# An mLSTM cell with a GELU feed-forward block: a later place for the second chunk's gates, a finer order on ScalarE, and one mask on GpSimd

## The chip, the cores and the metric

The kernel runs on one core of a Trainium2 chip. The core has five engines that run side by side, each through its own list of instructions in order: TensorE (PE in the profile; PEld is its loading of weights), VectorE (DVE), ScalarE (ACT), GpSimd (POOL), and SyncE (SP), which here issues nearly all DMAs. [...] The metric is the device time of one execution in microseconds (us); lower is better.

## The reference

The input is q, k, v and an output gate of shape (4 batches, 8 heads, 768 steps, 40), and two scalar gates per head and step. The reference walks over the steps:

```
m_new  = max(f + m, i)
f_stab = exp(f + m - m_new);  i_stab = exp(i - m_new)
C = f_stab * C + i_stab * outer(v, k);   n = f_stab * n + i_stab * k
y = sigmoid(o) * (C q) / max(|n.q|, 1)
```

Then y is put into rows of 320 (8 heads of 40) for 3072 tokens, and a feed-forward block follows: h = x @ w_in (320 x 2048), g = h * sigmoid(1.702 h), out = g @ w_out (2048 x 320). All is fp32.

## The kernel before

The 768 steps are cut into 6 chunks (w = 0 to 5) of L = 128 steps. Within a chunk the recurrence is turned into attention. From the gates come running sums and running maxima; from these an L x L matrix of weights per head, exp(...) below a causal mask; the scores k.q are multiplied by it (L352), and the product with v gives the values (L362). A state per head carries what came before the chunk. `seam` transposes a batch's rows to x (L404, L405); then come `up` (x @ w_in, GELU) and `down` (@ w_out). The loop over w at L761 does chunk w's feed-forward block and puts the attention of chunk w+1 between its matmuls.

The order is written by hand (`manual_schedule`): each engine gets its instructions in the order of the Python calls. PSUM tiles of the attention come from a pool of four (`ps_a`), so an instruction of TensorE can also wait until an older tile has been read.

Chunk 0 is special, since nothing runs beside it:

- `gates(w)` (L249) does the scan, the running maximum `m_run` and the columns derived from it on VectorE, on [32, 128] tiles. For w > 0 it also issues the DMA that writes `m_row` to DRAM (L269). For chunk 1 it is called at L686, after the transposes of batch 1. Its inputs are loaded by `load_gates(1)`, third in the list of first loads (L170).
- `weights(0, b)` (L319) builds the exponents in PSUM for four heads at a time: a matmul of the identity with `not_yet` puts a large negative number above the diagonal (L324), two small bf16 matmuls per head add the terms (L328, L329), and ScalarE takes the exponential (L330).
- `convert(n)` (L223) turns piece n of the weights, loaded as 64-bit words, into fp32: two ScalarE operations of 128 x 512 (L228 on the high words, L229 on the low ones) and four of VectorE (L232 to L237), the last of which needs L229. Pieces 0 to 9 are w_in, 10 to 19 w_out. The pieces pass through the rooms of `big`; `fetch(n)` issues their DMAs, and piece 16 takes the room of piece 10.

Chunk 1 and later take their weights by another way: `spread(w)` (L312) reads `m_row` back with four broadcasting DMAs of 512 KB into the `wt` tiles, ScalarE takes the exponentials (L334), and GpSimd masks them with `affine_select` (L336). `load_blocks(w, 0)` and `(w, 1)` load k and q in 16 small DMAs each, for VectorE's 32 x 32 transposes (L301).

`beside` (L744) says which pieces are converted and fetched ahead of which step of chunk 0's feed-forward block: pieces 9, 10, 11 are converted and piece 16 is fetched at j = 4. SP's DMAs take eight semaphores in turn, so that each one waits for the landing of the eighth before it.

Of the kernel before, what the change touches and what calls it, by code (L numbers as in the profile page):

```python
# [12 lines left out]
OP = mybir.AluOpType  # L13
# [9 lines left out]
L = 128  # L23
# [11 lines left out]
def kernel(  # L35
# [13 lines left out]
    B, H, S, D = q.shape  # L49
# [4 lines left out]
    NP = H // 2  # L54
# [20 lines left out]
    V, A, G, T = nc.vector, nc.scalar, nc.gpsimd, nc.tensor  # L75
# [80 lines left out]
    def fetch(n):  # L156
        if 6 <= n < 10:
            bits[n] = gp.tile([128, 512, 2], U32, tag="g", name="bits")
        else:
            room = xs if n == 19 else big[:, n if n < 6 else (n - 10) % 6, :]  # L160
            bits[n] = room.bitcast(U32).rearrange("p (a two) -> p a two", two=2)
        for r, c, src in pieces[n][1]:
            dst = bits[n][r, c].rearrange("p a two -> p (a two)")
            if len(src.shape) == 3:
                dst = dst.rearrange("p (j m) -> p j m", j=src.shape[1])
            nc.sync.dma_start(out=dst, in_=src)


    load_gates(0)
    for what, n in (("kq", 0), ("kq", 1), (load_gates, 1), ("vo", 0), ("vo", 1), ("kq", 2), (fetch, 0), ("kq", 3),  # L170
                    (fetch, 1), ("vo", 2), ("vo", 3), *((fetch, n) for n in range(2, 10))):
        if isinstance(what, str):
            load(0, what, slice(n, n + 1))
        else:
            what(n)
# [44 lines left out]
    kT, qT, wt, ys, xT, gs, o_ps, p_c = {}, {}, {}, {}, {}, {}, {}, {}  # L220


    def convert(n, engines="AV"):  # L223

        lo, hi, dst = bits[n][:, :, 0], bits[n][:, :, 1], pieces[n][0]
        dst_u = dst.bitcast(U32)
        if "A" in engines:
            A.activation(out=dst, in_=hi.bitcast(FP), func=AF.Abs)  # L228
            A.activation(out=lo, in_=lo, func=AF.Copy, scale=2.0 ** -29)  # L229
        if "V" not in engines:  # L230
            return
        V.tensor_scalar(out=dst, in0=dst, scalar1=HI_MIN, scalar2=HI_MAX, op0=OP.max, op1=OP.min)  # L232
        V.tensor_scalar(out=dst_u, in0=dst_u, scalar1=3, scalar2=0x3FFFFFFF, op0=OP.logical_shift_left,
                        op1=OP.bitwise_and)
        V.scalar_tensor_tensor(out=dst_u, in0=hi, scalar=0xC0000000, in1=dst_u, op0=OP.bitwise_and,
                               op1=OP.bitwise_or)
        V.tensor_tensor(out=dst_u, in0=dst_u, in1=lo, op=OP.add)  # L237
# [74 lines left out]
    def spread(w):  # L312

        for b in range(B):
            x = wt[w, b] = work.tile([L, NP, 2, L], FP, tag="wt", bufs=4, name="wt")
            nc.sync.dma_start(out=x.rearrange("s p i t -> s (p i) t"),
                              in_=m_row[w][b * H:(b + 1) * H, :].unsqueeze(0).to_broadcast([L, H, L]))

    def weights(w, b):  # L319
        if w == 0:  # L320
            x = wt[w, b] = work.tile([L, NP, 2, L], FP, tag="wt", bufs=4, name="wt")
            for i in range(2):
                pw = ps_a.tile([L, NP, L], FP, tag="a", name="p_w")
                T.matmul(pw, ident_bf, not_yet.unsqueeze(1).to_broadcast([L, NP, L]), start=True, stop=False)  # L324
                for p in range(NP):
                    h = b * H + 2 * p + i
                    one = pick[:, h:h + 1].to_broadcast([3 * BH, L])
                    T.matmul(pw[:, p, :], one, m3, start=False, stop=False)  # L328
                    T.matmul(pw[:, p, :], a3, one, start=False, stop=(p == NP - 1))  # L329
                A.activation(out=x[:, :, i, :], in_=pw, func=AF.Exp)  # L330
            return
        x = wt[w, b].rearrange("s p i t -> s (p i) t")
        for h in range(H):
            A.activation(out=x[:, h, :], in_=x[:, h, :], func=AF.Exp, scale=-1.0,  # L334
                         bias=cols[w][:, b * H + h:b * H + h + 1])
        G.affine_select(out=x, in_=x, compare_op=OP.is_ge, fill=0.0, base=0, pattern=[[0, H], [1, L]],  # L336
                        channel_multiplier=-1)
        if w > 1 and b == 0:
            gates_out(w)

# [58 lines left out]
    def seam(w, b):  # L399
        if b == 0:  # L400
            xT[w] = work.tile([128, 3, B, L], FP, tag="xT", bufs=1, name="xT")
        px = ps_a.tile([128, 3, L], FP, tag="a", name="p_x")
        for c in range(3):
            T.transpose(px[:, c, :], ys[w, b][:, c * 128:(c + 1) * 128], ident)  # L404
        A.copy(out=xT[w][:, :, b, :], in_=px)  # L405
# [277 lines left out]
    transposes(0, 0)  # L683
    weights(0, 0)
    transposes(0, 1)
    gates(1)  # L686
    scores(0, 0)
    weights(0, 1)
    scores(0, 1)
# [2 lines left out]
    values(0, 0)  # L692
    values(0, 1)
    transposes(0, 2)
    convert(0, "A")
    weights(0, 2)
    seam(0, 0)
    seam(0, 1)
    convert(0, "V")
    scores(0, 2)  # L700
    convert(1, "A")
    transposes(0, 3)
    weights(0, 3)
    convert(1, "V")
    scores(0, 3)
# [17 lines left out]
    values(0, 3, states=True)  # L723
    full_rows(0, 0, 0)
    full_rows(1, 0, 0)
    convert(2, "A")
    seam(0, 2)
    full_rows(0, 1, 0)
    seam(0, 3)
# [17 lines left out]
    def weights_in(n):  # L747
        done, ahead = beside.get(n, ((), ()))
        for p in done:
            convert(p)  # L750
        for p in ahead:
            fetch(p)

# [7 lines left out]
    for w in range(NW):  # L761
        more = w + 1 < NW
        for j in range(NF // 2):
            if w == 0 and j == 0:
                for pair_ in range(2):
                    for i, g in enumerate(hidden_of(0, pair_)):
                        A.activation(out=g, in_=first[pair_][i], func=AF.Gelu_apprx_sigmoid)
                    if pair_ == 0:
                        weights_in(0)
            elif w == 0 and j % 2 == 0:  # L770
                weights_in(j // 2)
                up(j, j == 2)
            elif w and j % 4 == 0:
                up_fast(w, j, next_keys if more and j == 0 else None)
            if w == 0 and j == 0:
                load_blocks(1, 0)
                fetch(15)
                spread(1)
                load_blocks(1, 1)
            if w == 1 and j == 3:  # L780
                weight_sums(3)
            if more:
                if w and j == 0:
                    load(w + 1, "o")
                if j == 4:
                    load(w + 1, "v")
                    if w:
                        spread(w + 1)
                    else:
                        fetch(17)  # L790
                        load(1, "o")
                if j == (4 if w else 6):
                    load(w + 1, "k")
                if w and j == 3:
                    for b in range(2, 4):
                        transposes(w + 1, b)
            if w and j in (3, 7):
                hidden_sums(w, 0, (j // 4 * 2, j // 4 * 2 + 1), 1, 2)
                if j == 3:
                    hidden_sums(w, 0, (0, 1), 3, 4)  # L800
        side = attention(w + 1) if more else []
        if w == 0:

            blocks = [(lambda b=b, n=n: down(w, b, n)) for ns in ((0, 1), (2,), (3,)) for b in range(B) for n in ns]
            stops = (0, 1, 5, 6, 8, 10, 12, 14, 15)
        else:
            blocks = down_fast(w, 0) + down_fast(w, 1)
            stops = (0, 1, 2, 4, 8, 10, 11, 12)
        for i, block in enumerate(blocks):
            if w == 0:  # L810
                weights_in(4 + i)
                if i == 0:
                    load_gates(2)
                if i == 2:
                    for b in range(B):
                        transposes(1, b, slice(0, 1))
                    first_sums((0, 1))
                    for b in range(B):
                        transposes(1, b, slice(1, 2))
                if i == 10:  # L820
                    load_blocks(2)
            elif w + 2 < NW and i == 0:
                load_gates(w + 2)
                load_blocks(w + 2)
            block()
            if i in stops and side:
                run(side.pop(0))
            if w == 1 and i == 1:
                weight_sums(2)
            if w:  # L830
                for at, c, *what in ((0, 0, (2, 3), 3), (1, 0, (2, 3), 4), (1, 1, range(4), 1),
                                     (5, 1, range(2), 2), (6, 1, range(2, 4), 2), (7, 1, range(4), 4)):
                    if i == at:
                        hidden_sums(w, c, *what)
                if i == 2 and not more:
                    hidden_sums(w, 1, range(4), 3)
            elif i == 11:
                weight_sums(0)
                weight_sums(1)
# [30 lines left out]
```

## Time and profile before

| | us |
|---|---|
| median of 6 runs | 485.79 (485.68 to 488.32) |
| profiled execution, its own time | 485.75 |
| its span | 484.0 |
| TensorE, ScalarE, VectorE, GpSimd busy | 478.1, 220.8, 342.4, 60.2 |
| SP issues chunk 1's first spread / the last load of its q | 56.76 / 71.71 |

The time of an execution is the span plus 1.75 us around it. A row of the timeline gives the start in us, the length, the engine, the line, the operation, output <- input and how many instructions are merged; brackets hold the idle time of the engine just before and what ended it. A row of the windows gives the stretch, its length, the busy time of PE, PEld, DVE, ACT and POOL with the number of instructions, TensorE's granted clock, the busy share of the DMA engines, and GB/s. A DMA's row shows how long SP took over issuing it; when it lands is told apart from that.

### The profile page before, as it was taken

How to read it: one execution, taken by the hardware profiler on the slowest of the kernel's cores; microseconds unless marked ns; L12 is line 12 of the kernel's file. 1: busy time of each engine (PE TensorE's matmuls, PEld its weight loads, DVE VectorE, ACT ScalarE, POOL GpSimd, SP SyncE). 2: the span in 40 equal slices, each digit the busy share in tenths (PEclk: the TensorE clock that was granted, in tenths of full speed). 3: DMA queues.
4: the chain of work that ended last, by engine and by line, in shares of the span. 5: the costliest groups of instructions: out<-in, count | busy, mean ns of one | idle time of the engine just before them, and what ended most of it. 6: DMA issues, size and time to landing. Idle time of an engine off the chain costs nothing. (4 is left out here: it accounts for less than half of the span.)

```text
span 484.0 us, 10433 instructions
## 1 busy us (share of the span) xinstructions
PE 478.1 (99%) x4072; PEld 396.9 (82%) x4072; DVE 342.4 (71%) x853; ACT 220.8 (46%) x575; POOL 60.2 (12%) x101
## 2 busy tenths in 40 slices
PE   8999999999999999999999999999999999999997
PEld 5874457777779999788999877999877999977997
DVE  7798879887978965667766677696576786254831
ACT  6767674503649302467600466900374920255300
POOL 3020001520001420000341000332000120000000
DMA  9999689954996000997000896200492000000000
GB/s 126 188 268 313 118 191 205 162 69 72 206 166 79 5 30 28 209 162 81 2 29 15 119 250 69 30 28 3 84 263 20 1 15 16 28 1 0 1 34 22
DMA packets 176097, 44.87 MB, mean 93 GB/s; under 512 B 164368, under 2 KB 169648, under 8 KB 176048
## 3 DMA queue, kind: packets, MB, share of 16 engines
q1 hardware_dynamic: 175472, 43.55, 48.8%
q8 instruction: 32, 0.52, 0.5%
q10 hardware_dynamic: 576, 0.66, 0.4%
q14 instruction: 17, 0.14, 0.1%
HBM read 40.17 MB, written 4.01 MB: 91 GB/s over the span
## 5 line engine op out<-in xcount | busy, mean ns | idle before, releaser
L615 PE MATMUL p_out<-w_out_sb,g 128*128 128x160 f32 x480 | 69.8, 301 | 0.0
L615 PEld LDWEIGHTS p_out<-w_out_sb,g 128*128 128x128 f32 x480 | 66.4, 190 | 0.9
L405 ACT COPY xT<-p_x 128x384 f32<-128x384 f32 x24 | 10.8, 481 | 121.0 <-PE p_x L404 108.0
L526 DVE TENSOR_TENSOR g<-p_u,g 128x256 f32<-128x256 f32 x80 | 33.6, 424 | 44.6 <-PE p_u L518 35.1
L523 ACT COPY g<-p_u 128x256 f32<-128x256 f32 x120 | 43.0, 376 | 43.6 <-PE p_u L518 39.3
L530 ACT ACTIVATE g<-g 128x256 f32<-128x256 f32 x120 | 42.3, 423 | 39.3 <-DVE g L526 39.3
L336 POOL TENSOR_SCALAR_AFFINE_SELECT wt<-wt 128x1024 f32<-128x1024 f32 x20 | 22.7, 1135 | 238.8 <-ACT wt L334 238.8
L620 DVE TENSOR_TENSOR o_sb<-o_sb,p_out 128x160 f32<-128x160 f32 x70 | 21.3, 316 | 42.3 <-PE p_out L615 41.9
L334 ACT ACTIVATE wt<-wt,cols 128x128 f32<-128x128 f32 x160 | 47.9, 391 | 0.0
L518 PE MATMUL p_u<-xT,w_in_sb 128*128 128x256 f32 x160 | 38.9, 382 | 0.0
L518 PE MATMUL p_u<-xs,big 128*128 128x256 f32 x160 | 37.9, 379 | 0.0
L546 PE MATMUL p_v<-xT,w_in_x 64*128 64x512 f32 x80 | 37.0, 602 | 0.0
L546 PE MATMUL p_u<-xT,w_in_x 64*128 64x512 f32 x80 | 37.0, 602 | 0.0
L566 PE MATMUL p_out<-w_out_sb,g 128*128 128x320 f32 x128 | 36.3, 436 | 0.0
L352 DVE TENSOR_TENSOR wt<-p_s,wt 128x512 f32<-128x512 f32 x48 | 30.4, 681 | 8.0 <-POOL wt L336 6.7
L615 PE MATMUL p_out<-t,big 128*128 128x160 f32 x240 | 35.5, 301 | 0.0
L518 PEld LDWEIGHTS p_u<-xT,w_in_sb 128*128 128x128 f32 x160 | 29.6, 190 | 5.4 <-DVE o_sb L620 1.5
L518 PEld LDWEIGHTS p_u<-xs,big 128*128 128x128 f32 x160 | 30.0, 190 | 4.6
L615 PEld LDWEIGHTS p_out<-t,big 128*128 128x128 f32 x240 | 33.3, 190 | 0.2
L566 PEld LDWEIGHTS p_out<-w_out_sb,g 128*128 128x128 f32 x128 | 23.8, 190 | 9.8 <-issue 0.5
L526 DVE TENSOR_TENSOR g<-p_v,g 128x256 f32<-128x256 f32 x80 | 29.8, 414 | 0.0
L546 PEld LDWEIGHTS p_v<-xT,w_in_x 64*128 64x128 f32 x80 | 14.2, 186 | 16.0 <-issue 16.0
(172 smaller groups left out, 856.7 us busy)
## 6 DMA issues: line engine op xcount, KB each, us to landing
wt<-m_row SPq DMA_DIRECT2D x20, 512.0 KB, 7.0
v_st<-in_v_dram SPq DMA_DIRECT2D x5, 640.0 KB, 8.9
eo<-in_o_gate_dram SPq DMA_DIRECT2D x5, 640.0 KB, 5.6
k_st<-in_k_dram SPq DMA_DIRECT2D x5, 640.0 KB, 11.2
out_dram<-o_sb SPq DMA_DIRECT2D x19, 160.0 KB, 1.8
big<-in_moe_w_in_dram SPq DMA_DIRECT2D x5, 512.0 KB, 7.1
k_bl<-in_k_dram SPq DMA_DIRECT2D x40, 64.0 KB, 2.8
q_bl<-in_q_dram SPq DMA_DIRECT2D x40, 64.0 KB, 2.6
```

The costliest lines, as they stand in the source:

```text
L334: A.activation(out=x[:, h, :], in_=x[:, h, :], func=AF.Exp, scale=-1.0, bias=cols[w][:, b * H + h:b * H + h + 1])
L336: G.affine_select(out=x, in_=x, compare_op=OP.is_ge, fill=0.0, base=0, pattern=[[0, H], [1, L]], channel_multiplier=-1)
L352: V.tensor_tensor(out=wt[w, b][:, :, i, :], in0=pw[i], in1=wt[w, b][:, :, i, :], op=OP.mult)
L405: A.copy(out=xT[w][:, :, b, :], in_=px)
L518: T.matmul(p[k][:, ts[t]], a[:, k // 2, k % 2 * 128:(k % 2 + 1) * 128], b, start=first, stop=True, skip_group_check=True)
L523: A.copy(out=g[k][i][:, ts[t]], in_=chain[k][:, ts[0]])
L526: V.tensor_tensor(out=g[k][i][:, ts[t]], in0=p[k][:, ts[pt]], in1=g[k][i][:, ts[t]], op=OP.add)
L530: A.activation(out=dst, in_=dst if src is None else src, func=AF.Gelu_apprx_sigmoid)
L546: T.matmul(p[k], w_in_x[r, k, :], x[r, 2, :], start=False, stop=True, skip_group_check=True)
L566: T.matmul(po, gs[w, f // 2][:, f % 2, b * L:(b + 1) * L], w_out_sb[:, f, :], start=(f == 0), stop=(f == NF - 1))
L615: T.matmul(po, a(f), b[:, f, :], start=(f == 0), stop=(f == NH - 1))
L620: V.tensor_tensor(out=dst, in0=x, in1=po, op=OP.add)
```

## The change

Four things. The loads of chunk 1's gates go from the third place of the first loads to their end, and `gates(1)` is called right after piece 9 is converted. `convert` knows three steps, H (high words) and L (low words) on ScalarE and V on VectorE; for pieces 0 and 1, H and L are put on the two sides of an exponential or of transposes. The mask of chunk 0's batch 1 is not a matmul any more but an `affine_select` of GpSimd on each half after the exponential. And `spread(1)` with the loads of q's blocks for chunk 1 moves from j = 0 to j = 4.

```diff
     load_gates(0)
-    for what, n in (("kq", 0), ("kq", 1), (load_gates, 1), ("vo", 0), ("vo", 1), ("kq", 2), (fetch, 0), ("kq", 3),
-                    (fetch, 1), ("vo", 2), ("vo", 3), *((fetch, n) for n in range(2, 10))):
+    for what, n in (("kq", 0), ("kq", 1), ("vo", 0), ("vo", 1), ("kq", 2), (fetch, 0), ("kq", 3),
+                    (fetch, 1), ("vo", 2), ("vo", 3), *((fetch, n) for n in range(2, 10)), (load_gates, 1)):
...
-    def convert(n, engines="AV"):
+    def convert(n, steps="HLV"):
...
-        if "A" in engines:
+        if "H" in steps:
             A.activation(out=dst, in_=hi.bitcast(FP), func=AF.Abs)
+        if "L" in steps:
             A.activation(out=lo, in_=lo, func=AF.Copy, scale=2.0 ** -29)
-        if "V" not in engines:
+        if "V" not in steps:
             return
...
+    def causal(x, n):
+
+        G.affine_select(out=x, in_=x, compare_op=OP.is_ge, fill=0.0, base=0, pattern=[[0, n], [1, L]],
+                        channel_multiplier=-1)
+
     def weights(w, b):
...
-                T.matmul(pw, ident_bf, not_yet.unsqueeze(1).to_broadcast([L, NP, L]), start=True, stop=False)
+                if b != 1:
+                    T.matmul(pw, ident_bf, not_yet.unsqueeze(1).to_broadcast([L, NP, L]), start=True, stop=False)
...
-                    T.matmul(pw[:, p, :], one, m3, start=False, stop=False)
-                    T.matmul(pw[:, p, :], a3, one, start=False, stop=(p == NP - 1))
+                    T.matmul(pw[:, p, :], one, m3, start=(b == 1), stop=False)
+                    T.matmul(pw[:, p, :], a3, one, start=False, stop=(b == 1 or p == NP - 1))
                 A.activation(out=x[:, :, i, :], in_=pw, func=AF.Exp)
+                if b == 1:
+                    causal(x[:, :, i, :], NP)
...
     transposes(0, 1)
-    gates(1)
     scores(0, 0)
...
-    convert(0, "A")
+    convert(0, "H")
     weights(0, 2)
+    convert(0, "L")
     seam(0, 0)
...
-    convert(1, "A")
+    convert(1, "H")
     transposes(0, 3)
+    convert(1, "L")
     weights(0, 3)
...
         for p in done:
             convert(p)
+            if p == 9:
+                gates(1)
         for p in ahead:
             fetch(p)
...
             if w == 0 and j == 0:
                 load_blocks(1, 0)
                 fetch(15)
+            if w == 0 and j == 4:
                 spread(1)
                 load_blocks(1, 1)
```

More of the change, by code (lines that the diff above doesn't have):

```diff
@@ L335, in weights @@
                          bias=cols[w][:, b * H + h:b * H + h + 1])
-        G.affine_select(out=x, in_=x, compare_op=OP.is_ge, fill=0.0, base=0, pattern=[[0, H], [1, L]],
-                        channel_multiplier=-1)
+        causal(x, H)
         if w > 1 and b == 0:
@@ L725 @@
     full_rows(1, 0, 0)
-    convert(2, "A")
+    convert(2, "HL")
     seam(0, 2)
```

## The prediction

> **What bounds the kernel now.** I read the page's parts 1 and 2 first, then the table of windows, then the timeline of the first 100 us, then SP's own timeline.
>
> ```profile
> span 484.0 us, 10433 instructions
> PE 478.1 (99%) x4072; PEld 396.9 (82%) x4072; DVE 342.4 (71%) x853; ACT 220.8 (46%) x575; POOL 60.2 (12%) x101
> ...
> DMA  9999689954996000997000896200492000000000
> ...
> 9.40:13.60 4.20, 4.09 (x51) 3.32 (x50) 2.94 (x10) 2.70 (x6) 0.00 (x0) 1.00 1.30 169
> 13.60:24.60 11.00, 10.59 (x158) 9.05 (x158) 9.64 (x23) 7.23 (x14) 0.47 (x2) 1.00 0.94 192
> 34.50:64.40 29.90, 29.90 (x144) 12.85 (x144) 25.18 (x47) 19.28 (x35) 0.16 (x1) 1.00 0.87 232
> 78.20:101.70 23.50, 23.50 (x225) 17.83 (x224) 20.60 (x38) 10.47 (x25) 6.61 (x8) 1.00 0.99 158
> ```
>
> TensorE (PE) is the bound: in the third and fourth window rows it is busy all the time. So the end moves by what the start gains, unless TensorE is made to wait later on. Only before about 25 us does TensorE follow the others. DMA is nearly full for the first 100 us (each digit of its row is 12 us).
>
> ```profile
> 8.86 0.41 DVE L254 TENSOR_TENSOR_SCAN f_run<-one,fi 32x128 f32<-32x128 f32 x1 [0.71 <-DMA fi<-in_f_gate_dram]
> 11.05 0.22 DVE L281 TENSOR_SCALAR dec_in<-pair,both 32x16 f32<-32x16 f32 x1
> 11.20 1.27 DVE L352 TENSOR_TENSOR wt<-p_s,wt 128x512 f32<-128x512 f32 x2
> 12.52 0.96 PEld L350 LDWEIGHTS p_s<-qT,kT 40*128 40x128 f32 x14 [0.30 <-DVE wt L352]
> 13.57 1.29 DVE L352 TENSOR_TENSOR wt<-p_s,wt 128x512 f32<-128x512 f32 x2 [1.11 <-PE p_s L350]
> 18.66 1.06 ACT L330 ACTIVATE wt<-p_w 128x512 f32<-128x512 f32 x2
> 20.84 1.29 DVE L352 TENSOR_TENSOR wt<-p_s,wt 128x512 f32<-128x512 f32 x2 [0.18 <-PE p_s L350]
> 24.48 1.29 DVE L352 TENSOR_TENSOR wt<-p_s,wt 128x512 f32<-128x512 f32 x2
> ```
>
> Columns: start, length, what, and in brackets the idle time before and who ended it. The eight gate instructions of chunk 1 fill VectorE from 8.86 to 11.27; the first product with the scores (ready at 10.55, when L350 ends) starts only then, and TensorE waits for the PSUM tile it frees. The four L352 pairs pace the head.
>
> ```profile
> 56.76 2.15 SPq L316 DMA_DIRECT2D wt<-m_row  x4
> 58.96 13.23 SPq L117 DMA_DIRECT2D q_bl<-in_q_dram  x16
> 72.29 1.38 SPq L166 DMA_DIRECT2D big<-in_moe_w_out_dram  x3
> ...
> 74.75 2.49 DVE L301 STREAM_TRANSPOSE qT<-q_bl 128x512 f32<-128x512 f32 x4 [0.52 <-DMA big<-in_moe_w_out_dram]
> 79.75 2.48 DVE L352 TENSOR_TENSOR wt<-p_s,wt 128x512 f32<-128x512 f32 x4
> ...
> 82.54 2.07 PE L362 MATMUL p_o<-v_st,wt 128*64 128x41 f32 x64
> ```
>
> SP issues in order and is never far ahead. The 16 loads of q for chunk 1 end at 72.20 and the last lands 2.5 us later by the trace, so their transposes wait. TensorE reaches the products of chunk 1 at 82.54 with 0.3 us of slack to the last L352 (82.23); the second batch's half starts 1.0 us later, so the slack of both is 1.3 us.
>
> **What the Trainium skill says.** "DMA: Bandwidth & Descriptors", section "Two DMAs through the same engine are not ordered": of two dependent DMAs the issuer must wait for the first one's semaphore. So SP must stand still between the write of m_row and the spreads that read it. In this trace that wait is free: the write of chunk 1 is issued at 30.51, lands 11.0 us later, and is read at 56.76. "GPSIMD Engine Reference", section 4.1 "Engine selection": a one-input operation is roughly at line rate on GpSimd; the trace agrees (L336, 128x1024: 1135 ns). "Perfetto Trace Analysis", section "Identifying the Most-Contended Engine": a matmul's busy share says little of roofline; I use it only to see where TensorE waits, which the 0.44 us of gaps in the second window row support.
>
> **The change part by part.**
>
> *Gates off the early queues.* Two loads (1.13 + 0.42 us of SP time at 4.54) go behind the tenth fetch. DMA is full there, so landings move only by the gates' own transfer. v_st lands 1.1 us after the q before it, with the gates between, against 0.95 us for its neighbours: I take 0.15 us (bounds 0 and 0.5). VectorE's 2.4 us go, and the first L352 can start at 10.65 instead of 11.20: 0.55 us.
>
> *Mask of batch 1.* It takes two L324 matmuls away from TensorE; each holds it for 0.22 us (7.09 to 7.31). GpSimd gets two selects of 128x512. From 1135 ns at 1024 and 290 at 128 elements: about 0.65 us each (with contention up to 1.0). The exponentials end at about 11.7 and 12.3, the selects at 12.4 and 13.0. The program order lists another PSUM wait too: the second score tile of batch 1 now waits for an exponential, not for L352. So scores end at about 12.8, and the second L352 pair ends at about 14.2 rather than 14.86: 0.6 to 0.7 us. Costed at nothing for GpSimd, which is idle from 6.97 to 16.40; should the selects take 1.0 us, this gain falls to 0.2.
>
> *Split conversions.* The same instructions, in another order. For batch 2 the exponentials move ahead of the low half (L229, 0.58 us): scores ready about 0.6 + 0.6 earlier, but VectorE's conversion then waits for the low half, ending at 20.0 instead of 20.66; the third L352 pair starts at 20.0 to 20.2 (0.6 to 0.8 us gained). For batch 3 ScalarE's run H, copy, copy, L, exponentials is as long as before and begins when the second piece has landed (issued 13.41, 7.1 us to landing: 20.5, now 20.4). Exponentials end at 23.8 instead of 23.9, VectorE's conversion at 23.7, so the last L352 pair starts at 23.7 to 23.9 instead of 24.48. Values and the seam follow it. **Gain of the head: 0.6 us** (bounds 0.2 and 1.0, the latter all the TensorE slack in the two window rows, 0.1 + 0.4, plus the mask matmuls).
>
> *Gates behind the tenth conversion.* 2.4 us of VectorE at about 50.7. The conversions after it have 1.27 us of idle at 57.26 and 1.83 at 66.25 (3.1 in all), so piece 15 is still on time. Nothing; if that cover went, the conversions of w_out would be late by at most 2.4, against a need at 67 and later.
>
> *SP's queue.* New order after the 16 loads of k: piece 15, m_row, piece 16 (three DMAs), spread, 16 loads of q, v. Each DMA also waits, in both programs, for the landing of the eighth before it (eight semaphores in turn). m_row goes out at 56.8, behind piece 15, whose second part landed 4.8 us after its issue at 56.23, at 61.0. An idle queue gave 1.5 us (chunk 2). So m_row lands between 58.3 and 61.3; I take 61. SP stands until then, and the first spread starts 4.3 us later than 56.76. What is behind it: 3 spreads, 16 loads of q, v, all in order. Not all of 4.3 passes on. Piece 16 (0.5 MB) crosses during the wait instead of after q. The spreads' 2 MB need 5.4 us (16 engines, 170 ns for 4 KB by the trace's packets), from about 62.3 to 68, where they ended at 66.7; q's loads, held before until 66.4, go on at 67 to 68.5 and then take 0.53 us each. So q is complete 0.6 to 2.2 us late; I take 1.0. v then starts without piece 16 ahead of it and is not late.
>
> *What is late next.* VectorE transposes q (2.5 us), converts piece 16 (2.44), does the L352 of batches 0 and 1 (2.48), all in order. Late by 1.0 against 1.3 us of slack, with TensorE arriving 0.6 early: TensorE waits 1.0 - 1.3 + 0.6 = 0.3 us. **Sum: -0.6 + 0.3 = -0.3 us.** In the profiled run's terms 485.75 - 0.3 = 485.4; the median is 485.79, the same within 0.04. After 114 us instructions and queues are as before and only shifted.
>
> **The rivals.**
>
> *SP's wait passes on in full.* Place: SP between m_row and the spread. If the spreads shift by 4.3 and nothing is caught up, q is 4.3 late and TensorE loses 4.3 - 1.3 = 3.0 us: 488.8. It decides from a lateness of 2.8 us, which costs 1.5. For it: the DMA row shows no room, and m_row once needed 11.0 us. Against: that was behind ten whole pieces; the backlog here is one piece and a few q/k loads (2.5 us to landing).
>
> *Nothing is left.* Selects of 1.0 us or the landing of the second piece hold the head, or q is late by just 1.3: 485.75. For it: the last exponentials move by 0.1 only. Against: VectorE, not ScalarE, was last before the fourth L352.
>
> *The head gains more.* TensorE's modelled ends hide waits and the new PSUM order removes them too: 1.6 us and no wait later, 484.1. Against: 0.5 us of visible gaps plus 0.44 of matmuls.
>
> *GpSimd's mask is the new wait throughout* (the change does the opposite of easing batch 1): bounded above by two selects at 1.0 us, within the second rival.
>
> **How the numbers follow.** A run of this kernel tells about 0.3% (1.46 us) from no change. Forecast (-0.3, own range 484.9 to 486.3): 0.56. Nothing left: 0.18, also within 0.3%. SP's wait, from 2.8 us late on: 0.17, slower. More head: 0.09, faster. So same 0.74. Predicted time 485.4. The range 484.4 to 487.4 takes the forecast, the second rival, half of the third's and a part of the first's cases, up to q 3.0 us late.
>
> **What would show it.** Right: first L352 at 10.6 to 10.8; two GpSimd selects ending before 13.2; fourth L352 pair at 23.7 to 23.9; m_row landing near 61 and the first spread right after; q's transposes at 75.3 to 76.5; the values of chunk 1 (82.54 before) at 82.0 to 82.6. Wrong: a fourth L352 at 24.4 (no head gain); transposes of q at 77.5 or later, with TensorE idle ahead of L350 or L362 (SP's wait dominates); any wait of TensorE between 35 and 64 us, or one after 114 us that is not there now.

## The result: slower by 0.6%

| | before | changed |
|---|---|---|
| median, us | 485.82 (35 runs, 485.67 to 488.32) | 488.78 (17 runs, 485.61 to 491.09) |
| ratio of the times, 95% interval | 1 | 1.0056 [1.0042, 1.0069] |
| profiled execution / its span, us | 485.75 / 484.0 | 488.15 / 486.4 |

The forecast was 485.4, no change. The time is 3.0 us above before, and no longer steady: the middle half of the runs lies between 488.15 and 489.85, against 485.75 to 485.96 before. In the listings after the change L352 is L360, L362 is L370, L350 is L358, L301 is L302, L316 is L317, L336 is L322 and L330 is L337.

The page and the table of windows of the changed kernel, in the columns of before:

```profile
span 486.4 us, 10426 instructions
PE 478.3 (98%) x4070; PEld 397.2 (82%) x4070; DVE 342.9 (70%) x853; ACT 220.4 (45%) x575; POOL 61.6 (13%) x103
...
DMA  9999689945996100997000796200392000000000
...
9.40:13.60 4.20, 4.20 (x73) 3.84 (x74) 2.03 (x4) 2.58 (x6) 1.22 (x2) 1.00 1.30 161
13.60:24.60 11.00, 9.73 (x138) 8.29 (x134) 8.80 (x21) 7.08 (x14) 0.47 (x2) 1.00 0.89 180
34.50:64.40 29.90, 29.90 (x146) 12.91 (x145) 26.39 (x54) 19.52 (x35) 0.16 (x1) 1.00 0.82 207
78.20:101.70 23.50, 22.24 (x217) 16.82 (x216) 20.98 (x41) 10.35 (x25) 6.61 (x8) 1.00 1.04 172
```

TensorE's busy time is the same as before to 0.2 us, so 2.4 us of span are waiting. The rows say where: 1.27 us idle in 13.6 to 24.6 (0.41 before) and 1.26 us in 78.2 to 101.7 (none before). In the window between them, 34.5 to 64.4, TensorE is full as it was. The first place is the head, from its timeline (start, length, what, idle time before and who ended it):

```profile
10.66 1.29 DVE L360 TENSOR_TENSOR wt<-p_s,wt 128x512 f32<-128x512 f32 x2 [2.50 <-PE p_s L358]
11.88 1.22 POOL L322 TENSOR_SCALAR_AFFINE_SELECT wt<-wt 128x512 f32<-128x512 f32 x2 [4.90 <-ACT wt L337]
12.85 1.29 DVE L360 TENSOR_TENSOR wt<-p_s,wt 128x512 f32<-128x512 f32 x2 [0.91 <-PE p_s L358]
19.87 1.28 DVE L360 TENSOR_TENSOR wt<-p_s,wt 128x512 f32<-128x512 f32 x2
21.45 0.66 ACT L228 ACTIVATE w_in_sb<-big 128x512 f32<-128x512 f32 x1 [1.69 <-DMA big<-in_moe_w_in_dram]
22.63 0.38 PE L331 MATMUL p_w<-xs 128*128 128x512 bf16 x1 [1.20 <-ACT kT L311]
25.06 1.29 DVE L360 TENSOR_TENSOR wt<-p_s,wt 128x512 f32<-128x512 f32 x2 [0.48 <-PE p_cols L286]
```

Three product pairs come 0.5 to 1.0 us earlier, about as forecast; the fourth is 0.6 us later. ScalarE stands 1.69 us for piece 1, the copy of kT is queued behind that, and TensorE needs the PSUM tile which the copy frees. The second place is chunk 1, from SP's, VectorE's and TensorE's timelines:

```profile
57.23 0.37 SPq L270 DMA_DIRECT2D m_row<-m_run  x1
57.70 1.32 SPq L166 DMA_DIRECT2D big<-in_moe_w_out_dram  x3
60.57 2.59 SPq L317 DMA_DIRECT2D wt<-m_row  x4
63.22 13.40 SPq L117 DMA_DIRECT2D q_bl<-in_q_dram  x16
...
78.49 2.49 DVE L302 STREAM_TRANSPOSE qT<-q_bl 128x512 f32<-128x512 f32 x4 [3.67 <-DMA q_bl<-in_q_dram]
83.34 2.48 DVE L360 TENSOR_TENSOR wt<-p_s,wt 128x512 f32<-128x512 f32 x4
...
79.26 2.06 PE L358 MATMUL p_s<-qT,kT 40*128 40x128 f32 x32 [0.40 <-DVE qT L302]
84.08 0.32 PE L370 MATMUL p_o<-v_st,wt 128*64 128x41 f32 x4 [0.42 <-DVE wt L360]
84.78 2.21 PE L370 MATMUL p_o<-v_st,wt 128*64 128x41 f32 x60 [0.37 <-DVE wt L360]
```

SP has issued piece 16 at 59.02, then stands until m_row has landed (60.5) and issues the first spread at 60.57, 3.8 us later than before. The last load of q is out at 76.62 (72.19 before), and the transposes of q start 3.74 us later than before. TensorE waits for them and for what follows from them.

The two places add up. TensorE's first matmul on w_in, which ends the head, starts at 27.35 (26.77 before): +0.58. From there to the end it takes 459.05 us (457.23 before): +1.82. Of these 1.82 us the trace shows 1.26 as idle time; the rest shows as no wait, since the ends of matmuls are modelled. The slack that the prediction found in chunk 1, 1.3 us, gives the same: q is 3.74 late, TensorE itself 0.58, so it should wait 3.74 - 1.3 - 0.58 = 1.86.

### The profile page after: what moved, and what is told of

Its sections match the earlier page's. It is cut to its first block, busy times and chain, and to the rows that moved or that the text cites. A ratio compares the mean times of both kernels' runs of the same rounds, so it can differ in the third digit from the quotient of the medians.

```text
span 486.4 us, 10426 instructions
## 1 busy us (share of the span) xinstructions
PE 478.3 (98%) x4070; PEld 397.2 (82%) x4070; DVE 342.9 (70%) x853; ACT 220.4 (45%) x575; POOL 61.6 (13%) x103
## 5 line engine op out<-in xcount | busy, mean ns | idle before, releaser
L413 ACT COPY xT<-p_x 128x384 f32<-128x384 f32 x24 | 10.8, 482 | 120.1 <-PE p_x L412 107.0
L322 POOL TENSOR_SCALAR_AFFINE_SELECT wt<-wt 128x1024 f32<-128x1024 f32 (+1 forms) x22 | 24.0, 1091 | 246.3 <-ACT wt L343 211.5
L360 DVE TENSOR_TENSOR wt<-p_s,wt 128x512 f32<-128x512 f32 x48 | 30.3, 682 | 10.0 <-POOL wt L322 6.0
L370 PEld LDWEIGHTS p_o<-v_st,wt 128*64 128x64 f32 x768 | 24.2, 138 | 4.2 <-issue 2.0
```

Of the source, the lines that this page charges most:

```text
L360: V.tensor_tensor(out=wt[w, b][:, :, i, :], in0=pw[i], in1=wt[w, b][:, :, i, :], op=OP.mult)
L370: T.matmul(po[b][t, h, :], wt[w, b][:, p, i, t], v_st[:, b * H + h, :], start=True, stop=True)
```

## The experiments

Theory Q: SP's wait for m_row's landing holds up q's loads. Rival H: the head loses by itself. Rival S: the new order of the queue (piece 16 ahead of the spreads), not the wait. In the table "q out" is the time from the issue of piece 15 to the end of the issue of q's 16 loads (0.5 us more than the issue of the last one, which the expectations give); "qT" is the start of q's transposes; "head" the start of the first w_in matmul; "rest" the span after it. These four come from one profiled execution of each kernel, the ratio from all its timed runs, beside runs of before on the same chip. "Low clock" counts the runs in which TensorE's mean granted clock was 0.998 or less (for before, over all the sets of runs beside the experiments).

| run | ratio | q out | qT | head | rest | low clock |
|---|---|---|---|---|---|---|
| before | 1 | 16.4 | 74.75 | 26.77 | 457.2 | 2 of 253 |
| changed | 1.0056 [1.0042, 1.0069] | 20.4 | 78.49 | 27.35 | 459.1 | 7 of 17 |
| after_again | 1.0072 [1.0053, 1.0091] | 21.0 | 79.89 | 28.82 | 459.0 | 3 of 6 |
| e1_head_only | 1.0002 [0.9993, 1.0010] | 16.8 | 76.30 | 27.65 | 458.8 | 0 of 22 |
| e2_gates_only | 1.0066 [1.0046, 1.0086] | 21.4 | 78.74 | 26.75 | 460.0 | 2 of 6 |
| e4_early_row | 1.0003 [0.9991, 1.0014] | 16.5 | 74.17 | 26.79 | 457.3 | 0 of 13 |
| e4_again | 1.0011 [1.0003, 1.0020] | 19.9 | 75.69 | 26.54 | 458.1 | 3 of 19 |
| e5_no_wait | 1.0018 [1.0008, 1.0028] | 20.3 | 77.23 | 27.28 | 457.9 | 2 of 22 |
| e6_piece16_behind | 1.0040 [1.0024, 1.0057] | 18.7 | 74.38 | 27.01 | 457.3 | 1 of 22 |
| e7_neither | 1.0055 [1.0030, 1.0080] | 19.5 | 77.59 | 27.66 | 458.5 | 1 of 8 |
| e8_piece16_ahead | 1.0009 [0.9999, 1.0018] | 18.5 | 77.17 | 27.65 | 457.7 | 2 of 22 |
| e10_gpsimd_queue | 1.0008 [1.0000, 1.0017] | 18.7 | 74.78 | 26.27 | 457.4 | 1 of 22 |
| c1_before_reads_q | 0.9991 [0.9974, 1.0009] | 16.8 | 75.24 | 27.07 | 457.7 | 0 of 14 |
| e12_reads_gate | 1.0029 [1.0011, 1.0048] | 19.5 | 76.97 | 26.81 | 458.1 | 6 of 22 |
| f1_write_added | 1.0012 [1.0003, 1.0020] | 18.1 | 74.75 | 26.19 | 457.9 | 1 of 22 |
| f2_loads_last | 1.0019 [1.0011, 1.0027] | 18.3 | 77.45 | 26.98 | 459.7 | 1 of 21 |
| h1_piece1_early | 0.9989 [0.9975, 1.0002] | 17.5 | 74.94 | 26.84 | 458.8 | 0 of 14 |
| e9_both_early | 1.0001 [0.9991, 1.0010] | 20.2 | 74.82 | 26.65 | 458.0 | 1 of 14 |
| b1_changed_mended | 0.9998 [0.9978, 1.0019] | 19.5 | 77.36 | 28.46 | 457.4 | 3 of 14 |
| b2_before_mended | 0.9972 [0.9960, 0.9984] | 10.0 | 74.08 | 26.67 | 457.4 | 1 of 22 |

One profile is one execution: e6's took 486.04 us beside a median of 488.56, e1's 488.12 beside 485.85. Where a profile and the ratio disagree, the ratio counts.

### The change in two halves

e1 keeps the split conversions and the mask, and puts back the gates, their loads and the spread. e2 is the opposite.

```diff
 e1:
-            if p == 9:
-                gates(1)
...
     transposes(0, 1)
+    gates(1)
     scores(0, 0)
...
                 fetch(15)
-            if w == 0 and j == 4:
                 spread(1)
                 load_blocks(1, 1)
```

> The head's two edits alone (split conversions, batch 1's mask by GpSimd); gates of chunk 1, their loads, spread and q's loads where they were before. Theory Q (the loss is SP's queue: it stands for m_row, and q's 16 loads are behind it): no loss, 485.2 to 485.8, because the queue is that of before. Rival H (the head itself loses, through piece 1 landing later or the mask): 486.2 or more, the fourth product pair of the head at 24.9 or later.

> The other half alone: loads of chunk 1's gates last, gates behind piece 9, spread and q's loads at j = 4; no split, mask by TensorE. Theory Q: slower by as much as the whole change or more, 488 to 489.5, transposes of q at 77.5 to 79, and a wide spread of the times. Rival H: 485.8 to 486.5.

The whole loss is in e2 (1.0066); e1 is not different from before. H falls as the cause of the loss. e1 also shows that the head's parts gain nothing that can be measured as they stand. Its profile shows a second place where lateness of the queue is paid:

```profile
88.81 1.27 ACT L350 ACTIVATE eo<-eo 128x1280 f32<-128x1280 f32 x1 [1.03 <-DMA eo<-in_o_gate_dram]
...
102.74 1.34 PE L574 MATMUL p_out<-w_out_sb,g 128*128 128x320 f32 x4 [1.03 <-DVE w_out_sb L238]
```

The output gate of chunk 1 lands late, VectorE stands behind it, and a piece of w_out is converted 1 us too late for TensorE.

### The write of m_row made early, and the wait taken away

e4 is the changed kernel, but the gates are loaded after the fourth v and o, computed at j = 0 ahead of k's loads, and the spread follows piece 15 as before: m_row lands about 7 us before SP reads it. e5 is the changed kernel with chunk 1's spread reading rows of q, so that SP has no landing to wait for; it does the same work, but chunk 1's values are then not the reference's.

```diff
 e4:
-                    ..., ("vo", 3), *((fetch, n) for n in range(2, 10)), (load_gates, 1)):
+                    ..., ("vo", 3), (load_gates, 1), *((fetch, n) for n in range(2, 10))):
...
             if w == 0 and j == 0:
+                gates(1)
                 load_blocks(1, 0)
                 fetch(15)
-            if w == 0 and j == 4:
                 spread(1)
                 load_blocks(1, 1)
```

> Changed kernel, but gates of chunk 1 computed at j = 0, ahead of k's 16 loads (their own loads behind those of v), so that m_row is written at about 44 and has landed when SP reaches the spread, which is back at j = 0. Theory Q: no stand of SP; transposes of q at 74.5 to 75.5; 485.0 to 485.6 with a narrow spread. Rival H: 487 or more, since the head is that of the changed kernel. Rival S (the spreads are slow by themselves once piece 16 and they stand close together): no test here, since piece 16 is behind q again.

> e4_early_row once more beside its variants: last q load issued at +16 after piece 15, ratio 0.999 to 1.001 by every theory of the queue. Should it come out at 1.002 or more, the first result was chance, and the other parts of the change cost something too.

> Changed kernel with the same DMAs of the same sizes in the same order, but chunk 1's spread reads 4 KB rows of q instead of m_row (chunk 1's weights are then computed from other numbers), so that SP has no landing of m_row to wait for. Theory Q: the first spread is issued at 58.5 to 59.5 instead of 60.6, q's transposes come 1.2 to 2.5 earlier than 78.5, and 486.0 to 487.5. If the order of the queue and not the wait is what costs (rival S), 488 to 489 as the changed kernel.

```profile
43.15 0.38 SPq L270 DMA_DIRECT2D m_row<-m_run  x1
53.74 0.91 SPq L166 DMA_DIRECT2D big<-in_moe_w_out_dram  x2
54.75 2.16 SPq L317 DMA_DIRECT2D wt<-m_row  x4
```

In e4 (SP's timeline) the first spread goes out 1.0 us after piece 15, q is out after 16.5 us, and the loss is gone: 1.0003, and 1.0011 on another chip. So gates at 43 us in place of 30 do no harm. The cost is in what e4 takes back: gates behind piece 9, m_row's write right ahead of the spreads, piece 16 ahead of them. e5 wins back about two thirds. Its queue is nevertheless as late as the changed kernel's (20.3), so the wait could not be all.

### The wait and piece 16, one at a time

In e6 piece 16 is fetched behind q's loads and the wait stays. e7 is e6 with e5's source. e8 is e4 with the spread and q's loads at j = 4, behind piece 16: that order without a wait.

```diff
 e6, e7:
-    beside = {..., 2: ((9, 10, 11), (16,)), ...
+    beside = {..., 2: ((9, 10, 11), ()), ...
...
                 spread(1)
                 load_blocks(1, 1)
+                fetch(16)
 e8 (against e4):
                 fetch(15)
+            if w == 0 and j == 4:
                 spread(1)
                 load_blocks(1, 1)
```

> The changed kernel once more, on the same chip as the three kernels beside it. All theories: ratio to before 1.004 to 1.007, last load of q about 20.4 us after piece 15 is issued (16.4 in the kernel before), transposes of q 22 to 24 us after it (19.0 before). What it adds is a second look at the head: if the landing of piece 1 is what spoiled the fourth product pair, TensorE's first w_in matmul (26.77 before, 27.35 in the first look at the changed kernel) follows ScalarE's start on piece 1 by 5.9 us again, whenever that start is.

> The changed kernel, but piece 16 is fetched behind q's loads, as in the kernel before; the write of m_row and SP's wait for its landing stay. All times here count from the issue of piece 15's first part. Theory W (the wait alone delays q): first spread at +4.1 to +4.4, last spread lands at +14 to +15, the last load of q is issued at +20, its transposes start at +22, ratio 1.004 to 1.007 like the changed kernel. Theory S (the half MB of piece 16 ahead of the spreads delays them, the wait is made up by a fuller queue): first spread at +4.1 too, but the last one lands at about +11.5, the last q load is issued at +17.2, transposes at +19.7, ratio 1.000 to 1.002. If both take part, halfway: +18.5 to +19, ratio 1.002 to 1.003.

> Both factors taken out of the changed kernel: piece 16 behind q's loads, and chunk 1's spread reads rows of q instead of m_row, so that SP does not wait for m_row and the values of chunk 1 are not the reference's. Every theory of the queue: first spread at +1.5, last q load issued at +16.4 to +17 after piece 15, transposes of q at +19 to +19.5, TensorE without a wait ahead of the scores and values of chunk 1, ratio 0.999 to 1.001. A ratio of 1.003 or more would say that neither the wait nor piece 16 matters, and that gates computed behind piece 9 or the other place in program order cost by themselves.

> Like e4_early_row (m_row written long before, so that SP never waits for it), but the spread and q's loads stand at j = 4 again, behind piece 16. This is the order without the wait, and its spread reads m_row, not rows of q as in e5 and e7. Times from the issue of piece 15. Theory W (the wait alone): as e4, last q load issued at +16 to +16.5, ratio 0.999 to 1.001. Theory S (piece 16 alone): last spread lands at +14 to +15, last q load at +19 to +20, ratio 1.004 to 1.007 as the changed kernel. Both add (what e6 suggests, +18.25 with the wait alone): spreads start at +2.5, the last lands at +12.5 to +13, last q load at +17.5 to +18.2, ratio 1.002 to 1.004.

The wait in e6, by windows of 1 us (last two numbers: busy share of the DMA engines, GB/s):

```profile
56.00:57.00 1.00, 1.00 (x4) 0.41 (x3) 0.96 (x3) 0.74 (x3) 0.00 (x0) 1.00 0.79 293
57.00:58.00 1.00, 1.00 (x4) 0.52 (x3) 0.83 (x2) 1.00 (x3) 0.00 (x0) 1.00 0.04 13
58.00:59.00 1.00, 1.00 (x3) 0.40 (x3) 0.97 (x3) 1.00 (x3) 0.00 (x0) 1.00 0.19 70
59.00:60.00 1.00, 1.00 (x4) 0.30 (x4) 0.96 (x2) 1.00 (x3) 0.00 (x0) 1.00 0.86 287
```

SP writes m_row at 54.57 and issues the next DMA at 57.77. Meanwhile the backlog runs dry, and for about 2 us all 16 DMA engines are nearly idle. e6 as a whole is at 1.0040. Piece 16 alone (e8) costs nothing measurable, 1.0009. Both together are the changed kernel: 1.0056 and 1.0072. By these three the wait would be the main cause. In the changed kernel piece 16 fills a part of the idle time, but then the spreads start while its half MB is still landing (until 62.4). (e8 also has the gates at j = 0; e10 below has them where the change put them.)

e7 contradicts this reading. It is e6 without the wait, beside it on the same chip, and no faster: 1.0055 [1.0030, 1.0080] against 1.0040 [1.0024, 1.0057], where every theory of the queue had said 0.999 to 1.001. It has eight runs only, and of the 2.2 us by which its profiled span exceeds that of before, 0.9 are lost in the head; 1.3 are lost behind it. So this pair gives the wait no share, while e5 gives it two thirds with piece 16 ahead: the wait's own share stays open.

### What e5 and e7 still pay

c1 gives the kernel before the source of e5. e12 gives the changed kernel another source, rows of f_gate (chunk 1's values are again not the reference's); the packets of its spreads have 512 bytes in place of 4 KB, so it changes more than the wait. f1 adds to e4 a write of 16 KB to DRAM, ahead of the spread, that nobody reads. f2 moves e4's loads of the gates to the end of the first loads.

```diff
 c1, e5, e7 (e12: f_gate[b, :, L:2 * L] in place of q's rows):
-                              in_=m_row[w][b * H:(b + 1) * H, :].unsqueeze(0)...
+                              in_=(m_row[w][b * H:(b + 1) * H, :] if w > 1 else q[b, 0]...).unsqueeze(0)...
 f1 (against e4):
                 fetch(15)
+                spare = rows.tile([BH, L], FP, name="spare")
+                nc.sync.dma_start(out=spare, in_=stacked[1][0:BH, :])
                 spread(1)
```

> The kernel before with one thing changed: chunk 1's spread reads rows of q instead of m_row (its values are then not the reference's). Theory N (q's rows are a slow source for a broadcast): 4 KB packets of the spread at 200 to 230 ns in place of 179, last spread lands at +12.5 to +14 after piece 15 (+11.0 before), ratio 1.002 to 1.005; then e5 and e7 say nothing of the wait. If the source is not to blame: ratio 0.999 to 1.001, and e7's 1.0055 speaks against the wait as the cause.

> The changed kernel with piece 16 ahead, the write of m_row still issued, but chunk 1's spread reads rows of f_gate (16 KB in all, like m_row), so that SP does not wait and chunk 1's values are not the reference's. Theory W (the wait is the cause): first spread at +2.4 to +3.4, last q load issued at +18 as in e8, ratio 1.000 to 1.002. If the wait is not the cause: last q load at +20, ratio 1.004 to 1.007.

> e4_early_row with one more DMA: a write of [32, 128] to DRAM, which nobody reads or waits for, between piece 15 and the spread, where the changed kernel has the write of m_row. Theory M (the write itself holds up what is behind it in the rings): last spread lands at +13 to +14, last q load issued at +18 to +19, ratio 1.002 to 1.004. If the write matters only through the wait for it: last q load 0.5 us later than in e4, ratio 1.000 to 1.0015.

> e4_early_row with the loads of chunk 1's gates at the end of the first loads, as in the changed kernel; the gates are still computed at j = 0, and m_row is written ahead of k's loads. Theory: the loads cost 0.3 us of SP's time wherever they stand, ratio 0.9995 to 1.0015. If they are the rest of the loss: VectorE waits for fi ahead of the gates and the conversions behind them are late, ratio 1.002 to 1.004.

The source is not to blame (c1, 0.9991), so e5 and e7 do speak of the wait, and e7 against it. Nor is the write by itself to blame (f1, 1.0012, as e4_again beside its own before). The loads at the end may cost 0.1% (f2 1.0019 against 1.0003 and 1.0011 for e4; the intervals touch). e12 lies at 1.0029, between the two forecasts. So without any wait between 0.2% and 0.55% remains in the three kernels that compute the gates behind piece 9, write m_row close ahead of the spreads and issue these ahead of q. What was not tried by itself is that place of the gates on VectorE. The profiles don't point there, since VectorE stands idle for q in all of them; and e10 and b1 below keep that place and lose little or nothing. e7:

```profile
57.22 2.15 SPq L317 DMA_DIRECT2D wt<-in_q_dram  x4
59.43 15.82 SPq L117 DMA_DIRECT2D q_bl<-in_q_dram  x16
...
77.59 2.49 DVE L302 STREAM_TRANSPOSE qT<-q_bl 128x512 f32<-128x512 f32 x4 [2.45 <-DMA big<-in_moe_w_out_dram]
```

In e7's SP timeline the spreads go out 1.5 us after piece 15, and still q takes 15.82 us to issue (13.23 before). The last spread's share landed on the first DMA engine 9.6 us after the issue of piece 15 and on the last one 4.2 us later; before, these were 9.3 and 1.7. e4_again shows the same straggling (9.6 and 4.7); its transposes of q still began at 75.69, within the slack, since its piece 15 went out 2 us earlier. Why an engine straggles in one execution and not in another stays open, and with it this part of the loss. In e12 a low clock of TensorE (last column, and the end of this document) adds to it in 6 of 22 runs; in e5 and e7 it is rare.

### The wait given to another engine

e10 is the changed kernel with one line changed: GpSimd issues chunk 1's spreads.

```diff
-            nc.sync.dma_start(out=x.rearrange("s p i t -> s (p i) t"),
+            (nc.gpsimd if w == 1 else nc.sync).dma_start(out=x.rearrange("s p i t -> s (p i) t"),
```

> The changed kernel with one line changed: chunk 1's four spreads are issued by GpSimd, which has nothing to do from 42 to 71 us, so that the wait for m_row's landing holds GpSimd and not SP; piece 16 stays ahead of q. Theory Q (what counts is what stands ahead of q's loads on SP's queue): q's first load goes out at +3 after piece 15, its last at +12 to +16, transposes of q at 74 to 76, TensorE without a wait at chunk 1's scores and values, ratio 0.999 to 1.001. Rival T (the traffic counts, not the order: the same bytes share the DMA engines): last q load at +19 to +20, ratio 1.004 to 1.007 as the changed kernel. A third way: GpSimd issues slowly and the spreads come later than ScalarE's exponentials of chunk 1 at 69 us; then TensorE waits for wt instead.

```profile
55.12 0.37 SPq L270 DMA_DIRECT2D m_row<-m_run  x1
55.60 1.32 SPq L166 DMA_DIRECT2D big<-in_moe_w_out_dram  x3
57.02 15.79 SPq L117 DMA_DIRECT2D q_bl<-in_q_dram  x16
58.26 2.36 POOL L317 DMA_DIRECT2D wt<-m_row  x4 [16.95 <-DMA m_row<-m_run]
...
77.71 2.06 PE L358 MATMUL p_s<-qT,kT 40*128 40x128 f32 x32
82.05 2.07 PE L370 MATMUL p_o<-v_st,wt 128*64 128x41 f32 x64
```

The bracket shows the same wait, now on an engine with nothing else to do; q's loads go out at once. Same gates, same place, same piece 16, same bytes: 1.0008 [1.0000, 1.0017]. What changed is that neither the wait nor the spreads stand ahead of q's loads on SP. This is the strongest evidence that the loss comes from what stands ahead of q in SP's queue. It doesn't tell the wait from the spreads behind it, since both left the queue together. T, that the traffic alone makes the delay, falls.

### The head, and a better version

h1 is e1 with piece 1 fetched ahead of k and q of batch 3; e9 does the same to e4. b1 is the changed kernel with that and e10's line. b2 is h1 with e10's line, so with the gates where they were before.

```diff
-                    ..., ("kq", 2), (fetch, 0), ("kq", 3), (fetch, 1), ("vo", 2), ...
+                    ..., ("kq", 2), (fetch, 0), (fetch, 1), ("kq", 3), ("vo", 2), ...
```

> The head's parts only (split conversions, mask of batch 1 on GpSimd; gates, their loads and the spread as before), with piece 1 fetched ahead of k and q of batch 3. Theory P (the landing of piece 1 decides when the head ends): ScalarE starts piece 1 without a wait for its DMA, at 19.5 to 20.4 instead of 20.9 to 22.2 in the four traces with the split, TensorE's first w_in matmul at 25.6 to 26.4 (26.77 before), ratio 0.998 to 0.9995. Rival K (k and q of batch 3 become as late as piece 1 was): TensorE waits for k_st or q_bl ahead of its transposes of batch 3, first w_in matmul at 26.8 or later, ratio 1.000 to 1.002.

> The version that the runs point to: e4_early_row with piece 1 fetched ahead of k and q of batch 3. Theory P (the landing of piece 1 ends the head): ScalarE starts piece 1 at 20.0 to 20.8, TensorE's first w_in matmul at 26.2 to 26.6 (26.77 before), no wait of TensorE at chunk 1's scores and values, ratio 0.998 to 0.9995. Rival: the head's gain is taken back by k and q of batch 3 or by the queue of chunk 1, as in h1; ratio 0.9995 to 1.001.

> The changed kernel with chunk 1's spreads on GpSimd's queue (as in e10) and piece 1 fetched ahead of k and q of batch 3. If the head's gain is real and nothing behind it takes it back: TensorE's first w_in matmul at 26.0 to 26.5 (26.77 before), no wait at chunk 1's scores and values, ratio 0.998 to 0.9995. If the queue of chunk 1 takes it back: 0.9998 to 1.001.

> The split conversions, the mask on GpSimd and piece 1 ahead of k and q of batch 3, with the gates where they were before and chunk 1's spreads issued by GpSimd at j = 0, so that q's loads follow piece 15 at once. q's first load goes out at +1, its transposes have 2 us more slack than before, and the scatter upward should be smaller. Ratio 0.998 to 0.9995 if that slack was what the slower executions lacked; 0.9998 to 1.001 if it was not.

Fetched early, piece 1 is there when ScalarE comes (no wait in h1, e9, b1, b2), but the head of h1, e9 and b2 ends at 26.65 to 26.84. ScalarE now waits 0.2 to 0.7 us for piece 0, and in b2 TensorE waits 0.42 us for q of batch 3, as rival K has it. That piece 1 delays piece 0 isn't shown: in e1, e5, e6, e7, e8 and after_again, with the fetches in the old order, ScalarE waits 0.8 to 1.2 us for piece 0 too. e10 and f1 end the head at 26.27 and 26.19, because piece 1 happened to land at 20.3 and 20.2 there. In ten of the thirteen traces with the split and the old order of fetches, the first w_in matmul follows ScalarE's start on piece 1 by 5.9 us (after_again, whose clock drops, needs 6.9). The changed head is as fast as its loads.

b2 is faster than both kernels: 0.9972 against before, median 485.65 beside 486.34. SP's timeline, and GpSimd's:

```profile
59.45 0.91 SPq L166 DMA_DIRECT2D big<-in_moe_w_out_dram  x2
60.45 9.03 SPq L117 DMA_DIRECT2D q_bl<-in_q_dram  x16
...
40.85 2.29 POOL L317 DMA_DIRECT2D wt<-m_row  x4 [11.53 <-DMA m_row<-m_run]
```

Here m_row is written at 29.93, and GpSimd issues the spreads as soon as it has landed, 16 us earlier than SP did. q follows piece 15 directly and is out at 69.48, although piece 15 went out 3.7 us later than before. A good part of the gain is slack and not speed: its fastest run is only 0.5 us below the fastest of before, but 21 of its 22 runs stay within 1.2 us of it, while nearly a quarter of before's runs on that chip were above 487.3. How much the head's parts add was not separated; with them alone h1 is at 0.9989 [0.9975, 1.0002].

## Why the prediction was wrong

- **Head, 0.6 us gain: half right.** First pair at 10.66 (10.6 to 10.8 forecast), the two selects 0.61 us each, ended at 13.10 ("before 13.2" forecast), third pair at 19.87 (20.0 to 20.2). The fourth was to come at 23.7 to 23.9 and came at 25.06. The step that failed is the landing of the second piece ("20.5, now 20.4"): it landed at 21.4, SP having taken 4.0 us over its issue instead of 3.0. That 1.0 us is nearly all of the 1.2 us by which the fourth pair missed; the copies and TensorE wait behind it. Where piece 1 did land at 20.2 to 20.3 (f1, e10), the fourth pair came at 23.90 and 23.98 and the head gained 0.5 to 0.6 us, as forecast. Why the landing varies is not shown.
- **Gates behind piece 9 at nothing:** in the changed kernel VectorE had the room (26.39 of 29.90 us busy, TensorE full). e10 and b1 agree; e5, e7 and e12 leave it open whether this place is free in every execution.
- **SP's queue, q 1.0 us late: wrong, and the larger part of the wrong sign.** The landing of m_row (61 forecast, 60.5 measured) and the start of the first spread (4.3 us later forecast, 3.8 measured) were right. The term that failed is the catching up. I let the spreads' 2 MB pass in 5.4 us, done at 68; the last landed at 71.0. The 5.4 us price the spreads' packets as if they had the 16 engines to themselves, but in both traces packets of other loads run between them. The trace of before already told it: from the issue of the first spread to the landing of the last it has 10.0 us (56.76 to 66.7). The forecast took 6.9 (61.1 to 68), and the changed kernel needed 10.4 (60.57 to 71.0). q's loads behind them still went out one per 0.53 us and caught up nothing. q's issue ended 4.4 us late, its transposes began 3.74 late, and TensorE lost 1.8 us where the sum had 0.3. I had taken piece 16 "crosses during the wait" as a saving: in e6, without it, the engines run nearly empty during the wait; with it, the spreads start while its half MB is still landing. v, "not late" in the forecast, landed 2.5 us late (82.8, before 80.3), but TensorE didn't wait for it.
- **Slack of 1.3 us: right.** With the lateness as measured it gives TensorE's loss in chunk 1 within 0.1 us in five traces: changed 1.86 (1.82 measured as rest), after_again 1.8 (1.8), e2 2.7 (2.7), e5 0.7 (0.7), e12 0.9 (0.9); not in e7 (0.65, 1.3) and f2 (1.2, 2.5), where more was late than q (in f2 TensorE waits 0.8 us for v). Nor is q all that can be late: in e1 and h1, within the slack, the rest is 1.5 us longer than before, and TensorE waits 1.03 and 0.78 us for a piece of w_out.
- **The rival with SP's wait, 488.8, was what happened** (488.78), from the place and beyond the deciding point (2.8 us) that it named. That the two numbers agree so closely is luck: the rival has 3.0 us of waiting in chunk 1, and the profile has 1.8 there, 0.6 in the head, and the rest of the median comes with a low clock (last section). Of its two grounds, that the DMA row shows no room was right; m_row's 11.0 us behind a backlog was not the reason, m_row took 3.3 us. The reason is that nothing behind it catches up.
- **Two readings were off, without effect:** the 2.5 us of the last q load count from its issue at 71.71, so that it landed at 74.2; and the gaps in the second window row are 0.41 us, not 0.44.

## What to carry to other kernels

When a DMA that reads what another DMA has written is moved closer to its write, ask which loads stand behind it in the same queue and what they feed: on a loaded in-order queue assume that the delay passes on in full. Catching up needs spare DMA time, and a wait ahead of it first drains what was there. Price a group of transfers by what it took in the trace beside its neighbours, not by its bytes alone. If such a wait must be, give it, with the transfers that depend on it, to an engine whose queue holds nothing that is due.

## What the runs showed of the hardware

- m_row's DRAM write of 16 KB took 2.8 to 3.3 us from issue to landing where it follows piece 15, and 10.6 to 12.2 us where it is written at about 30 us. In the first place it landed 0.2 us after the last part of piece 15, in all nine traces: its latency goes with what stands ahead in the queue.
- The 16 engines of a queue don't finish a broadcast DMA together: the last of the four spreads landed on its last engine 1.4 to 4.7 us after its first, from one kernel or execution to another. q's loads follow the last one: in all sixteen traces with 4 KB spreads ahead of them on SP, the issue of the fifth load ends 0.2 to 0.8 us before that landing, and the other eleven then go out one per 0.53 us.
- TensorE's granted clock has a part in the loss. In 7 of the changed kernel's 17 runs its mean was 0.998 or less, and their median is 490.08 us, beside 488.26 for the ten at full clock (of the 3.0 us that the median lost, 2.4 are thus the two waits, as in the profile). Where the profile shows such a drop, it is in the head; after_again, in windows of 2 us (third number from the end: the clock):

```profile
18.00:20.00 2.00, 0.97 (x9) 0.54 (x9) 1.16 (x3) 1.92 (x4) 0.00 (x0) 1.00 0.70 149
20.00:22.00 2.00, 2.00 (x22) 1.88 (x21) 1.86 (x4) 1.09 (x4) 0.00 (x0) 0.83 1.07 242
22.00:24.00 2.00, 2.00 (x13) 1.39 (x13) 1.70 (x4) 2.00 (x4) 0.00 (x0) 0.50 0.97 172
24.00:26.00 2.00, 2.00 (x26) 1.73 (x24) 0.95 (x2) 1.22 (x3) 0.00 (x0) 0.82 0.62 126
```

TensorE idles for 1.03 us, 2 us later its clock is halved for some 3.4 us, and the head ends at 28.82 (b1 alike: 28.46). The Trainium skill, "TensorE: Matmul & The Clock Gate", section "What's actually happening", has just these two states, half and full, set by how busy TensorE was in a window of about 3.4 us; the length and the 0.50 agree. The page lets the half state follow an idle window of that length; here no idle stretch in the head was longer than 1.03 us. e1 idled as long in the same 2 us and kept its clock, so what sets off the drop is not shown. Over all runs, kernels with chunk 1's gates in the head had a low clock in 3 of 325 runs (before, e1, h1, c1, b2), those without them in 34 of 250. So this goes with the gates' move, though why was not tried.
